# One written order replaced by another: squares and casts leave GpSimd, and one more output pair is made in seven products

## The chip, the cores and the metric

The kernel runs on one core of a Trainium2 chip. A core has five engines that run side by side: TensorE (PE in the profile) multiplies matrices, VectorE (DVE) and ScalarE (ACT) work element by element, GpSimd (POOL) does so too, more slowly, and starts DMAs, and SyncE (SP) does nothing here but start DMAs. Each engine works through its own list of instructions strictly in order; between engines, an instruction waits on semaphores until what it reads is there and what it overwrites is no longer needed. TensorE reads SBUF (the on-chip memory) and writes PSUM, eight banks of 2 KB in each of 128 partitions.

The metric is the device time of one execution in microseconds (us).

## The reference, cut to what matters

```
scores = q @ k.T / sqrt(64)                       # 8 batches, 12 heads, 448 positions, head size 64
attn   = maximum(scores, 0)**2 / 448
x      = (attn @ v), heads side by side           # 3584 tokens x 768
h      = x @ w_in                                 # 768 x 2048
out    = (h * sigmoid(1.702 * h)) @ w_out         # 2048 x 768, result 3584 x 768, float32
```

There is no softmax: a score is clipped at zero and squared, so the attention needs no row sums. All scale factors are put off: one factor 64*448 is divided out inside the activation of `h` and multiplied back when the activation is widened, and divided out again at the output.

## The kernel before, in words

**Units and groups.** The attention is cut into 24 units u = 0..23: three for each batch, four heads in each. The tokens are cut into eight groups g = 0..7 of 384 (even g) or 512 (odd g); a group's second stage can begin when the attention of its tokens is done. 128 tokens make a block m of the output; groups have three or four of them.

**The order is written out by hand** as one long string of words (line 466 on); `do` (line 441) reads a word and issues its instructions. The place of a word in the string sets the order on every engine and queue at once, since each engine takes its own instructions in the string's order. `:d`, `:a`, `:p` put a word on VectorE, ScalarE or GpSimd; without it the table `home` (line 439) decides, and what is not in the table is VectorE's. `@4.5` names the PSUM banks. The words that matter here:

- `Lk` `Lq` (line 97): load float32 k or q of a unit into `kst` or `qst` through SyncE; there is one buffer of each. `K` `Q` (line 107): cast it to 16 bit. `Rk` `Rq` (line 117): transposing DMA through SyncE into `kT`, `qT`. Units 0 to 5 are transposed on TensorE instead (`tk` `tq`, copied out by `ek` `eq`); for units 1 to 5 `jk` `jq` load and cast in one DMA through GpSimd. `V` loads v the same way (four buffers).
- `s u.j` (line 143): four score matmuls into two banks. `r u.j.a` (line 156): clip one bank into `at` (eleven buffers). `x u.j` (line 165): square `at`, 128 x 896, in place; both inputs of that product lie in SBUF. `a u` (line 173): 28 matmuls with v. `e` (line 189): copy the attention's result out as the group's input.
- `f g.f.r` (line 221): plain matmuls of the first layer (all of group 0, half of group 1), two at a time. `u g.i.n` (line 269): one of the seven products that make a 2 x 2 block of the first layer, six matmuls. `t`, `b` copy and add its partial sums, `g` applies the activation (ScalarE), `v` widens the result to 16 bit (line 216, GpSimd): the group's input of the second layer.
- `p g.m.n` (line 375): one of the seven products that make output blocks m and m+1, eight matmuls of 384 columns. `A g.m.n` (line 357) makes the sums of its left sides, `W c.n` (line 345) those of its right sides from `w_out`. `m` (line 337) makes half an output block plainly, 16 matmuls; `i` (line 399) does so with the weights that the sums have changed in place. `h`, `l`, `n` copy the results out, `o` stores them through SyncE.
- `S i.n` (line 245) and `T g.n` (line 259) make the sums for the first layer's products. `jwa` `jwb` (line 411) load `w_in` in four quarters of two halves, `jo` (line 415) loads `w_out`, all through GpSimd. `z` are matmuls of zeros at the start. `G3` (line 421) is a tiny copy on SyncE that waits for the last half but one of `w_in`, so that no `Lk`, `Lq` starts before it.

The sums with two operands (`tt`, line 87) are all on line 88, the widenings on line 217, the casts and copies on lines 79 to 85, the matmuls of the products on line 203.

Of the kernel before, what the change touches and what calls it, by code (L numbers as in the profile page):

```python
# [15 lines left out]
def kernel(  # L16
# [406 lines left out]
    with tc.manual_schedule():  # L423
# [15 lines left out]
        home = {"K": "a", "Q": "p", "r": "a", "t": "a", "h": "a", "v": "p"}  # L439
# [19 lines left out]
        def zeros(e, p, n):  # L459
# [8 lines left out]
            "Lk0 z13@0 jk1 V1 jq1 I V0 K0:d tk0@1 z1 ek0 jk2 Lq0 Q0:a tq0@2 eq0 tk1@3 s0.3@4.5 "  # L468
            "r0.3.1 jq2 ek1 s0.1@6.7 r0.1.0 r0.3.0:d s0.0@0.1 s0.2@2.3 tq1@5 r0.0.1:d r0.2.0 "
            "s0.5@4.6 r0.1.1 s0.4@1.2 r0.0.0 r0.5.1 s0.6@7.0 eq1 r0.4.0:d tk2@5 x0.0 s1.0@1.6 "  # L470
            "r0.4.1 x0.4 jwb2 r0.5.0 x0.5 r0.6.1 jk3 r0.2.1 r0.6.0 x0.3:p jq3 x0.1 ek2 r1.0.1 "
            "r1.0.0 x0.2 x0.6 s1.5@2.4 s1.2@0.3 r1.2.0 s1.1@7.6 r1.1.1 tq2@5 a0@1.0 r1.1.0 r1.5.0 "
            "s1.6@6.7 eq2 r1.2.1 x1.0 r1.5.1 r1.6.0 s1.3@5.2 r1.3.0 x1.1 x1.2 tk3@3 e0.0.0 "
            "e0.0.1:a jk4 x1.5 e0.1.0:a tq3@4 r1.3.1 ek3 eq3 jwb0 x1.3 jq4 jwa0 s1.4@6.5 r1.6.1 "
            "V2 x1.6 r1.4.1 r1.4.0 s2.0@1.3 s2.2@2.7 r2.2.1 e0.1.1:a s2.1@4.5 r2.0.1 r2.0.0 "
            "r2.2.0 tk4@6 r2.1.1 x1.4 a1@7.0 e1.0.1:a ek4 r2.1.0:d x2.2 s2.6@3.6 r2.6.0 tq4@1 "
            "r2.6.1 e1.0.0 s2.3@2.4 r2.3.0 e1.1.1 x2.0 x2.1 eq4 s2.4@5.0 r2.3.1 jwa1 s2.5@3.6 "
            "f0.2.0@2 r2.4.0 r2.4.1 jwb1 jwa2 jq5 f0.3.0@4 s3.0@1.5 x2.6 e1.1.0 x2.3 f0.3.1 x2.4 "
            "jk5 r2.5.0 r2.5.1 x2.5 r3.0.0:d S0.1 V3 f0.2.1 f0.0.0@7 f0.0.1 s3.1@0.3 r3.0.1 "
            "a2@6.5 jwb3 r3.1.1:d r3.1.0 s3.2@1.0 e2.0.0 f0.1.0@3 e2.0.1:a r3.2.1 r3.2.0 G3 "  # L480
            "e2.1.1:a e2.1.0 x3.0 f0.1.1 f0.1.2 g0.1 x3.1:p V4 f0.2.2 s3.5@6.0 r3.5.0:d g0.2 "
            "s3.4@1.5 f0.0.2 v0.1 f0.3.2 r3.4.0 V5 r3.4.1 f0.4.0@3 r3.5.1:d x3.2 x3.5 g0.3 g0.0 "
            "f0.4.1 s3.3@2.6 s3.6@1.0 jwa3 f0.8.0@5 r3.3.1 r3.6.0 v0.0 r3.3.0 f0.4.2 g0.4 f0.8.1 "
            "f0.8.2 s4.1@4.7 s4.3@6.1 r3.6.1:d s4.0@0.2 f0.6.0@3 f0.6.1 r4.1.0 r4.3.1 x3.6 V9 "
            "f0.6.2 r4.3.0 x3.3 f0.5.0@4 r4.1.1:d r4.0.1:d x3.4 f0.5.1 S0.2 x4.1 f0.5.2 v0.4 "
            "s4.2@7.1 x4.3 a3@2.6 g0.8 g0.5 r4.2.1:d s4.4@5.4 r4.2.0 r4.0.0 tq5@7 g0.6 v0.2 jo1.0 "
            "Lk6 r4.4.0:d r4.4.1 tk5@0 eq5 s4.5@1.3 s4.6@4.5 ek5 e3.0.1:a f0.11.0@6 x4.2:a "
            "f0.7.0@7 f0.11.1 f0.11.2 r4.6.1:d r4.5.0 r4.5.1:d r4.6.0:d f0.10.0@0 f0.10.1 f0.7.1 "
            "x4.6 e3.0.0:a jo0.0 x4.5:a x4.4 f0.10.2 S2.1 g0.11 s5.1@1.5 s5.0@2.3 x4.0:p v0.5 "
            "f0.7.2 v0.11 f0.14.0@4 r5.0.1:d v0.6 f0.14.1 g0.10 r5.1.0 r5.1.1 r5.0.0 f0.14.2 "  # L490
            "jo0.1 S1.1 g0.14 g0.7 s5.4@6.0 a4@1.3 s5.3@5.2 r5.4.0:d v0.7 r5.3.0 e4.0.0:a "
            "s5.2@4.7 r5.4.1:d r5.2.1:d f0.12.0@6 x5.0:p e4.0.1:a f0.13.0@0 r5.2.0:d f0.12.1 "
            "f0.12.2 x5.4:a g0.12 v0.3 f0.15.0@5 f0.15.1 s5.5@7.1 r5.5.1 s5.6@4.3 r5.3.1:d x5.3 "
            "r5.5.0:d r5.6.0:d f0.13.1 r5.6.1 jo1.1 f1.7.0@2 f0.13.2 f1.1.0@6 x5.1:p v0.12 v0.10 "
            "v0.14 K6:p x5.5:a g0.13 f0.15.2 f1.5.0@1 f1.5.1 f1.7.1 S2.2 S2.4 x5.2:a x5.6:a "
            "f0.9.0@7 f0.9.1 f0.9.2 f1.4.0@3 S2.3 g0.15 g0.9 a5@4.0 e5.0.1:a f1.0.0@5 f1.0.1 "
            "f1.3.0@7 f1.1.1 Lq6 Q6:a e5.0.0 T1.1 T1.2 S1.2 v0.13 f1.7.2 g1.7 f1.3.1 v1.7 v0.9 "
            "Lq7 f1.3.2 f1.4.1 f1.4.2 f1.5.2 Rk6 u1.2.0@0 f1.6.0@4 Rq6 S3.1 g1.5 f1.6.1 g1.3 "
            "f1.2.0@2 f1.0.2 f1.6.2 v1.3 v0.15 t1.2.0 S3.3 g1.0 v0.8 g1.6 v1.0 Lk7 T1.4 S3.2 g1.4 "
            "u1.2.2 S3.4 W2.1 f1.2.1 f1.2.2 S1.4 u1.3.0@1 v1.4 W1.1 Q7:a f1.1.2 g1.1 v1.5 v1.1 "  # L500
            "u1.2.1@7 b1.2.1 g1.2.1 v1.2.1 v1.6 m0.0.0@5 u1.2.3 g1.2 s6.2@4.3 T1.3 Lq8 t1.3.0 "
            "s6.1@6.2 u1.3.2 S0.3 t1.2.2 n0.0.0:a r6.2.0 u1.2.4 r6.1.1:d r6.2.1:d s6.0@5.4 r6.0.1 "
            "r6.0.0 x6.0:a t1.3.2 V11 t1.2.4:d W0.1 u1.3.1@2 W2.2 Rq7 W0.2 m0.0.1@3 K7:p Q8:a "
            "b1.3.1 b1.2.3 g1.2.3 Rk7 u1.2.5 u1.2.6 u1.3.4 r6.1.0 W3.1 S0.4 v1.2 V7 u1.3.3 g1.2.5 "
            "v1.2.3 s6.4@4.5 s6.3@6.0 S1.3 n0.0.1 t1.3.4 g1.3.1 b1.2.6 b1.3.3 s6.5@3.7 r6.4.0 "
            "u1.3.5 x6.1:p r6.3.0:d r6.4.1:d r6.5.0 W1.2 v1.3.1 v1.2.5 u1.3.6 Lk8 g1.3.5 W3.2 V6 "
            "x6.4:a r6.3.1:d x6.2:a r6.5.1 Rq8 b1.3.6 K8:p m0.1.0@4 s6.6@6.3 W2.4 v1.3.5 g1.3.3 "
            "v1.3.3 s7.2@5.1 g1.2.6 x6.3 W1.4 v1.2.6 Lq9 g1.3.6 s7.0@0.2 r7.2.1 r7.0.0 x6.5:a Q9 "
            "r6.6.1:d r7.2.0:d Lk9 r7.0.1 m0.1.1@7 r6.6.0:d n0.1.0:a Rk8 s7.1@3.1 x6.6 W3.4 "
            "x7.0:a a6@5.0 s7.3@6.2 r7.1.0:d r7.1.1 n0.1.1 Lq10 s7.4@4.3 x7.2 e6.0.1:a K9:p "  # L510
            "r7.3.1 e6.1.1:a e6.0.0 r7.4.0:d p1.0.0@1 o0.0 r7.4.1:d e6.1.0:a s7.6@7.2 s7.5@0.5 "
            "r7.3.0 x7.1 x7.3 r7.6.0 r7.6.1:d r7.5.0 s8.2@4.6 m0.2.0@3 r7.5.1 r8.2.0:d V10 x7.4 "
            "s8.1@7.0 x7.6 r8.2.1 x7.5:a h1.0.0 n0.2.0:a s8.0@5.6 r8.1.1 a7@2.4 v1.3.6 r8.0.1 "
            "A1.0.1@0 A1.0.2@1 s8.3@3.0 W0.4 r8.3.0 r8.1.0:d e7.0.1 e7.1.1:a r8.3.1 p1.0.1@6 "
            "s8.5@7.3 V8 e7.0.0:a r8.0.0:d x8.1 e7.1.0 r8.5.0:d Rk9 r8.5.1 Rq9 s8.6@4.5 x8.0 x8.2 "
            "r8.6.1 x8.3:a p1.0.2 x8.5 r8.6.0:d s8.4@0.2 r8.4.1 s9.0@3.7 r8.4.0 l1.0.1 r9.0.0 "
            "x8.6 r9.0.1 x8.4 x9.0:a m0.2.1@5 n0.2.1:a s9.1@2.4 A1.0.4 r9.1.1:d Lk10 r9.1.0 "
            "a8@0.3 s9.2@7.5 e8.0.0:a Q10:d e8.0.1:a s9.3@4.2 r9.2.1:d r9.3.1 K10:p p1.0.3 "
            "u2.0.0@5 r9.2.0 Rk10 u2.1.0@2 Lk11 K11:p T2.1 W3.3 e8.1.0 T2.2 T2.3 e8.1.1:a "
            "s9.4@7.3 u2.0.1@0 W1.3 r9.4.1:d t2.0.0 u2.0.2 b2.0.1 t2.1.0 u2.1.2 u2.1.1@3 r9.3.0:d "  # L520
            "b2.1.1 W0.3 T2.4 r9.4.0 t2.0.2 u2.0.3 u2.0.4 g2.0.1 v2.0.1 t2.1.2 u2.2.0@7 g2.1.1 "
            "t2.0.4 b2.0.3 Lq11 t2.2.0 v2.1.1 u2.1.4 t2.1.4 h1.0.2 x9.2 u2.1.3 b2.1.3 u2.2.1@4 "
            "u2.0.6 g2.0.3 v2.0.3 b2.2.1 x9.4:a u2.2.2 u2.1.6 b2.0.6 g2.2.1 g2.0.6 Rq10 W2.3 "
            "u2.2.3 u2.3.0@0 Q11:a b2.1.6 t2.2.2:d u2.0.5 v2.0.6 g2.1.6 u2.3.1@3 g2.1.3 t2.3.0:d "
            "b2.3.1 v2.1.6 v2.2.1 u2.2.4 u2.1.5 u2.3.2 u2.3.3 t2.2.4 u2.2.5 A1.0.3 b2.2.3 u2.2.6 "
            "Lk12 o0.1 g2.3.1 t2.3.2 v2.3.1 v2.1.3 g2.0.5 g2.1.5 v2.0.5 u2.3.4 p1.0.4 g2.2.3 "
            "g2.2.5 s9.6@5.2 v2.1.5 b2.2.6 s9.5@4.7 t2.3.4:d u2.3.5 x9.1:a v2.2.3 K12 Lq12 b2.3.3 "
# [147 lines left out]
```

## Time and profile before

Four executions took 369.32, 369.71, 372.15 and 372.30 us; the median is 370.93. The profiled one is the third.

| | profiled execution |
|---|---|
| device time | 372.15 us |
| span from the first to the last instruction | 370.4 us |
| granted TensorE clock | 0.994 of full speed |
| PE busy | 356.9 us, 3570 matmuls |
| DVE busy | 289.3 us, 519 instructions |
| ACT busy | 277.1 us, 542 instructions |
| POOL busy | 179.0 us, 229 instructions |
| DMA | 51.39 MB |

Busy time counts when at least one instruction of the engine is under way; neighbours on one engine overlap at their ends, so an instruction's own duration is longer than the step from one to the next. A row "A 0.55" of the timeline gives the start and then the time until the end. Matmuls are pipelined, so PE is shown busy also where matmuls trickle; the step from the start of one batch of matmuls to the next tells more than its busy share.

### The profile page before, as it was taken

The numbers are of one execution on the slowest core, as the hardware profiler recorded it, in microseconds if no ns is written. First come the engines' busy times: TensorE is split into PE (matmuls) and PEld (weight loads), VectorE is DVE, ScalarE is ACT, GpSimd is POOL, SyncE is SP. The second block draws the span as 40 slices with busy tenths as digits, with TensorE's granted clock in tenths as the row PEclk, the third lists the DMA queues.
The fourth block names the chain that finished last, engine by engine and source line by source line (L and its number), as shares of the span: only waits on it lengthen the run. The fifth ranks groups of instructions, "written<-read, shape, count | busy, mean of one in ns | idle before, by whom it ended". The sixth has DMA issues, their size and how long they took to land.

```text
span 370.4 us, 9086 instructions
## 1 busy us (share of the span) xinstructions
PE 356.9 (96%) x3570; PEld 231.0 (62%) x3570; DVE 289.3 (78%) x519; ACT 277.1 (75%) x542; POOL 179.0 (48%) x229
## 2 busy tenths in 40 slices
PE   7689999999999999999999999999999999999994
PEld 3344554674559655786559655786549755787662
DVE  4879997499998777878899678766887899764642
ACT  3968985688788988878977997888995897175310
POOL 6745685766213587257403765368342546043300
PEclk9989999999999999999999999999999999999999
DMA  9999999698984895978494396356934042300244
GB/s 197 184 202 186 213 208 191 159 193 198 132 158 112 187 254 99 162 166 193 96 195 89 95 170 165 101 141 152 245 88 88 2 112 27 87 0 2 64 118 118
DMA packets 65227, 51.39 MB, mean 139 GB/s; under 512 B 35744, under 2 KB 61856, under 8 KB 65184
## 3 DMA queue, kind: packets, MB, share of 16 engines
q1 hardware_dynamic: 48256, 36.32, 41.1%
q0 software_dynamic: 16608, 14.09, 26.2%
q8 instruction: 28, 0.46, 0.5%
q10 hardware_dynamic: 320, 0.39, 0.4%
q14 instruction: 15, 0.12, 0.1%
HBM read 45.61 MB, written 11.01 MB: 153 GB/s over the span
## 4 chain that ended last, share of the span: by engine, by line
PE 86%; DVE 6%; DMA 4%; POOL 2%; issue 1%; ACT 0%; SPq 0%; POOLq 0%; DVEq 0%; ACTq 0%
PE hx L203 29%; PE ox L203 26%; PE sc L150 9%; PE av L181 7%; PE ht L228 7%; PE os L203 4%; PE op L203 3%; DMA q<-in_q_dram 2%; DVE at L161 2%; DVE wT L88 1%; DVE at L88 1%; DMA qst<-in_q_dram 1%; PE tr L131 1%; DVE asum L88 1%; POOL at L88 1%
## 5 line engine op out<-in xcount | busy, mean ns | idle before, releaser
L163 ACT ACTIVATE at<-sc 128x448 f16<-128x448 f32 x215 | 105.0, 559 | 15.7 <-PE sc L150 15.4
L161 DVE TENSOR_SCALAR at<-sc 128x448 f16<-128x448 f32 x121 | 71.6, 616 | 12.9 <-PE sc L150 12.3
L217 POOL TENSOR_SCALAR go<-gf 128x512 f16<-128x512 f32 x64 | 41.3, 645 | 63.6 <-ACT gf L214 46.8
L88 DVE TENSOR_TENSOR gf<-hx,gf 128x512 f32<-128x512 f32 (+1 forms) x78 | 47.9, 626 | 26.8 <-PE hx L203 14.2
L203 PEld LDWEIGHTS <-win 128*128 128x128 f16 x624 | 56.4, 98 | 8.4 <-issue 2.8
L88 POOL TENSOR_TENSOR at<-at 128x896 f16<-128x896 f16 x27 | 45.8, 1700 | 30.8 <-ACT at L163 18.7
L217 POOL TENSOR_SCALAR ge<-gf 128x384 f16<-128x384 f32 x64 | 35.9, 561 | 46.1 <-ACT gf L214 28.9
L169 ACT ACTIVATE at<-at 128x896 f16<-128x896 f16 x57 | 53.9, 955 | 0.9 <-DVE at L161 0.6
L150 PE MATMUL sc<-qT,kT 64*64 64x448 f16 x672 | 51.3, 362 | 1.4 <-DVE at L161 0.6
L88 DVE TENSOR_TENSOR at<-at 128x896 f16<-128x896 f16 x84 | 51.9, 651 | 0.8 <-ACT at L163 0.4
L214 ACT ACTIVATE gf<-gf 128x512 f32<-128x512 f32 (+1 forms) x78 | 43.2, 580 | 9.4 <-DVE gf L88 9.3
L203 PE MATMUL ox<-wout,go 128*128 128x384 f16 x256 | 46.5, 327 | 0.0
L203 PEld LDWEIGHTS <-winS 128*128 128x128 f16 x468 | 42.6, 98 | 4.5 <-issue 1.0
L203 PEld LDWEIGHTS <-go 128*128 128x128 f16 x320 | 29.9, 98 | 22.6 <-issue 4.8
L203 PEld LDWEIGHTS <-ge 128*128 128x128 f16 x288 | 27.5, 98 | 19.7 <-issue 3.3
L79 ACT ACTIVATE gf<-hx 128x512 f32<-128x512 f32 (+1 forms) x51 | 27.3, 543 | 15.2 <-PE hx L203 7.2
L203 PE MATMUL hx<-T,winS 128*128 128x256 f16 (+1 forms) x312 | 37.0, 260 | 0.0
L181 PE MATMUL av<-at,v 64*64 64x448 f16 x672 | 36.6, 354 | 0.1
L150 PEld LDWEIGHTS <-kT 64*64 64x64 f16 x672 | 17.6, 105 | 25.9 <-issue 20.6
L203 PE MATMUL hx<-xo,win 128*128 128x256 f16 x252 | 32.1, 273 | 0.0
L203 PE MATMUL ox<-wT,asum 128*128 128x384 f16 x176 | 31.8, 327 | 0.0
L203 PEld LDWEIGHTS <-asum 128*128 128x128 f16 x200 | 18.7, 98 | 15.3 <-issue 3.1
(78 smaller groups left out, 482.6 us busy)
## 6 DMA issues: line engine op xcount, KB each, us to landing
out_dram<-osb SPq DMA_DIRECT2D x52, 192.0 KB, 3.2
kst<-in_k_dram SPq DMA_DIRECT2D x19, 448.0 KB, 4.7
qst<-in_q_dram SPq DMA_DIRECT2D x19, 448.0 KB, 4.0
v<-in_v_dram POOLq DMA_DIRECT2D x24, 224.0 KB, 5.4
win<-in_moe_w_in_dram POOLq DMA_DIRECT2D x8, 384.0 KB, 11.0
wout<-in_moe_w_out_dram POOLq DMA_DIRECT2D x4, 768.0 KB, 12.5
k<-in_k_dram POOLq DMA_DIRECT2D x5, 224.0 KB, 8.3
q<-in_q_dram POOLq DMA_DIRECT2D x5, 224.0 KB, 9.0
```

Of the source, the lines that this page charges most:

```text
L79: nc.scalar.activation(out=o, in_=i, func=AF.Copy)
L88: eng[e].tensor_tensor(out=o, in0=x, in1=y, op=op)
L131: nc.tensor.matmul(out=ps[64 * a:64 * a + 64, j * 128:(j + 1) * 128], lhsT=x[:, a, 64 * j:64 * j + 64], rhs=ident[:, :], is_transpose=True)
L150: nc.tensor.matmul(out=sc[a][c, 0:S], lhsT=st["kT"][r, j, c], rhs=st["qT"][r, :, c], start=True, stop=True)
L161: nc.vector.tensor_scalar(out=o, in0=i, scalar1=0.0, scalar2=None, op0=ALU.max)
L163: nc.scalar.activation(out=o, in_=i, func=AF.Relu)
L169: nc.scalar.activation(out=at, in_=at, func=AF.Square)
L181: nc.tensor.matmul(out=av[s][64 * a:64 * a + 64, 0:S], lhsT=v16[r, a, 64 * j:64 * j + 64], rhs=at[r, a, :], start=(j == 0), stop=(j == J - 1))
L203: nc.tensor.matmul(out=o, lhsT=lhs(i), rhs=rhs(i), start=start and i == 0, stop=i == n - 1, skip_group_check=True)
L214: nc.scalar.activation(out=o, in_=i, func=AF.Gelu_apprx_sigmoid, scale=1.0 / SC)
L217: eng[e].tensor_scalar(out=o, in0=i, scalar1=SC, scalar2=1.0, op0=ALU.mult, op1=ALU.mult)
L228: nc.tensor.matmul(out=hp[g, f][:, 0:n], lhsT=w[:, i, fo:fo + 128], rhs=xts[g][:, i, 0:n], start=i == 0, stop=i == NK - 1)
```

## The change

Nothing of the functions is changed, only the string of words, and one entry of `home`: a `Q` without an engine is ScalarE's. Over the whole string:

| | before | after |
|---|---|---|
| squares `x` on ScalarE, VectorE, GpSimd | 57, 84, 27 | 62, 106, 0 |
| casts `K` on ScalarE, VectorE, GpSimd | 6, 1, 12 | 16, 3, 0 |
| casts `Q` on ScalarE, VectorE, GpSimd | 8, 1, 10 | 16, 3, 0 |
| clips `r` on ScalarE, VectorE | 215, 121 | 223, 113 |
| copies `e` on ScalarE, VectorE | 40, 32 | 35, 37 |
| `h` on ScalarE, VectorE | 20, 13 | 23, 13 |
| `l` on ScalarE, VectorE | 6, 38 | 3, 45 |
| `n` on ScalarE, VectorE | 9, 3 | 4, 4 |
| plain half blocks `m`, `i` | 6, 6 | 0, 8 |
| products `p` and sums `A` | 77, 47 | 84, 52 |

All other words are there as often as before. The 128 widenings and all of GpSimd's DMAs stay where they were. The six `m` were group 0's three output blocks; now blocks 0 and 1 are seven products `p0.0.n`, and block 2 is two `i`. The order of nearly all words is new. The core of the diff (the opening, the last quarter of `w_in`, the first products of group 0 with unit 6 and 7 beside them, and the casts of units 17 and 18):

```diff
-        home = {"K": "a", "Q": "p", "r": "a", "t": "a", "h": "a", "v": "p"}
+        home = {"K": "a", "Q": "a", "r": "a", "t": "a", "h": "a", "v": "p"}
...
-            "Lk0 z13@0 jk1 V1 jq1 I V0 K0:d tk0@1 z1 ek0 jk2 Lq0 Q0:a tq0@2 eq0 tk1@3 s0.3@4.5 "
-            "r0.3.1 jq2 ek1 s0.1@6.7 r0.1.0 r0.3.0:d s0.0@0.1 s0.2@2.3 tq1@5 r0.0.1:d r0.2.0 "
-            "s0.5@4.6 r0.1.1 s0.4@1.2 r0.0.0 r0.5.1 s0.6@7.0 eq1 r0.4.0:d tk2@5 x0.0 s1.0@1.6 "
...
-            "f0.4.1 s3.3@2.6 s3.6@1.0 jwa3 f0.8.0@5 r3.3.1 r3.6.0 v0.0 r3.3.0 f0.4.2 g0.4 f0.8.1 "
...
-            "u1.2.1@7 b1.2.1 g1.2.1 v1.2.1 v1.6 m0.0.0@5 u1.2.3 g1.2 s6.2@4.3 T1.3 Lq8 t1.3.0 "
-            "s6.1@6.2 u1.3.2 S0.3 t1.2.2 n0.0.0:a r6.2.0 u1.2.4 r6.1.1:d r6.2.1:d s6.0@5.4 r6.0.1 "
-            "r6.0.0 x6.0:a t1.3.2 V11 t1.2.4:d W0.1 u1.3.1@2 W2.2 Rq7 W0.2 m0.0.1@3 K7:p Q8:a "
...
+            "jq1 Lk0 K0:d I jk1 Lq0 jwb2 Q0:a z13@0 tk0@1 jk2 ek0 tq0@2 tq1@3 eq0 s0.6@4.5 eq1 "
+            "s0.1@6.7 r0.1.0:d jq3 s0.3@1.2 z1 r0.3.1:d jq2 r0.6.0 tk1@3 s0.4@0.4 jk3 r0.6.1 V0 "
+            "r0.1.1:d r0.3.0 s0.0@6.5 r0.0.1 s0.2@2.1 r0.2.0:d ek1 r0.0.0 s1.1@7.5 jwa0 tk2@6 "
+            "r0.4.1 s1.0@2.4 r0.2.1 x0.3 x0.0 x0.6 s0.5@3.1 r1.1.1:d x0.1:a r0.4.0 x0.2 r1.1.0 "
...
+            "f0.8.0@4 e2.1.1 x3.3 r3.1.0:d f0.8.1 f0.8.2 V4 s4.1@5.1 s3.5@6.0 e2.1.0:a g0.2 g0.8 "
+            "s3.6@3.2 x3.1 r4.1.1:d r4.1.0 r3.5.0 f0.4.0@7 f0.6.0@4 s4.3@1.5 r3.5.1:d r3.6.0 "
+            "r3.6.1 r4.3.1:d s3.4@6.0 x3.5:a f0.6.1 v0.8 r3.4.1:d r3.4.0:d f0.4.1 x3.4 f0.6.2 "
+            "f0.4.2 x3.6:a g0.6 tq5@3 tk5@2 eq5 s4.2@5.0 V5 ek5 s4.0@6.4 g0.4 r4.0.1:d r4.2.1 "
+            "r4.2.0 r4.0.0:d a3@3.7 s4.5@2.0 s4.4@5.4 S0.1 v0.2 jwa3 f0.10.0@6 f0.10.1 jo1.0 "
+            "r4.4.1:d x4.2:a e3.0.1 f0.10.2 r4.5.0 r4.4.0 r4.3.0 x4.4 e3.0.0:a s4.6@2.4 r4.6.1:d "
+            "x4.1 S3.1 s5.2@5.7 r5.2.0 g0.10 r4.5.1 f0.7.0@1 x4.3 v0.6 jo0.0 f0.11.0@3 f0.7.1 "
+            "v0.1 f0.7.2 x4.0 r5.2.1 jo0.1 f0.5.0@5 f0.5.1 s5.1@4.6 g0.7 v0.7 s5.4@0.7 x4.5:a "
+            "r5.1.0:d f0.5.2 r5.4.1:d Lk6 r4.6.0 x4.6 f0.11.1 f0.11.2 f0.13.0@1 f0.13.1 s5.0@4.2 "
...
+            "S3.3 v1.2 v1.3 v1.5 u1.2.2 A0.0.1@0 W2.1 W3.1 W3.2 W0.1 Rk6 f1.0.1 f1.0.2 p0.0.0@1 "
+            "K7 g1.0 u1.3.0@3 s6.0@0.4 g1.6 W3.4 W2.2 W1.1 s6.2@2.7 t1.2.2 T1.3 Lq8 u1.2.4 v1.6 "
+            "h0.0.0 b1.2.1 W2.4 r6.0.1 t1.3.0 v1.4 W1.2 t1.2.4 r6.2.1 Q8 r6.0.0 r6.2.0 v1.0 W1.3 "
+            "p0.0.1@4 W3.3 u1.2.5 u1.2.3 u1.3.2 u1.3.1@7 s6.1@0.2 W0.2 g1.2.5 A0.0.2@1 g1.2.1 "
+            "W2.3 v1.2.1 b1.2.3 g1.2.3 t1.3.2 Lk8 r6.1.0 b1.3.1 u1.2.6 v1.2.5 r6.1.1 l0.0.1 Lq7 "
+            "b1.2.6 p0.0.2 Q7 W1.4 Rk7 s6.5@6.0 S0.3 s6.3@5.2 r6.5.0 W0.3 Rq8 u1.3.3 x6.0:a K8 "
+            "A0.0.3 r6.5.1:d r6.3.0:d u1.3.4 Rq7 t1.3.4:d r6.3.1 h0.0.2 x6.2 g1.3.1 p0.0.3 W0.4 "
+            "s6.6@6.0 s6.4@5.2 r6.4.1:d b1.3.3 r6.6.1 r6.4.0 x6.3 p0.0.4 v1.3.1 V8 x6.5:a A0.0.4 "
+            "h0.0.4 l0.0.3 u1.3.5 u1.3.6 g1.3.5 v1.3.5 b1.3.6 g1.3.3 p0.0.5 Lq9 x6.1 Lk9 s7.4@0.2 "
+            "r6.6.0 x6.6 x6.4 g1.2.6 s7.0@5.3 p0.0.6 s7.2@6.7 l0.0.5:a g1.3.6 r7.4.0 r7.0.0:d "
+            "r7.0.1:d r7.4.1 l0.0.6 r7.2.1 s7.1@1.0 r7.2.0 r7.1.0:d r7.1.1 v1.3.6 Rk8 x7.0 a6@5.2 "
...
+            "u4.0.0@7 t4.0.0:d u4.1.0@4 r15.2.0:d u4.2.0@2 u4.0.1@5 Lq17 T4.4 u4.0.2 t4.1.0 "
+            "h3.0.2 u4.1.1@1 T4.3 x15.0 b4.0.1 t4.0.2 u4.1.2 b4.1.1 Lk18 A3.2.1@0 u4.0.4 g4.1.1 "
+            "e14.1.0 t4.1.2 u4.0.3 t4.0.4:d Q17 g4.0.1 K18 Rk16 v4.1.1 x15.3 p3.0.4 b4.0.3 Lk19 "
```

Of the two casts in the last piece, `Q17` was GpSimd's before and stood apart from its load, and `K18` was ScalarE's.

## The prediction

> **What bounds the kernel now.** I read the page first, then TensorE's timeline, because the page's busy share of PE is no measure of work.
>
> ```profile
> span 370.4 us, 9086 instructions
> ...
> PE 356.9 (96%) x3570; PEld 231.0 (62%) x3570; DVE 289.3 (78%) x519; ACT 277.1 (75%) x542; POOL 179.0 (48%) x229
> ...
> PE 86%; DVE 6%; DMA 4%; POOL 2%; issue 1%; ACT 0%; SPq 0%; POOLq 0%; DVEq 0%; ACTq 0%
> ```
>
> The chain of waits runs through PE for 86% of the span. Starts in PE's timeline give the step of each batch:
>
> ```profile
> 77.64 0.82 PE L203 MATMUL hx<-T,win 128*128 128x256 f16 x6
> 78.30 0.82 PE L203 MATMUL hx<-xo,winS 128*128 128x256 f16 x6
> ...
> 91.06 0.54 PE L150 MATMUL sc<-qT,kT 64*64 64x448 f16 x5
> 91.87 0.38 PE L150 MATMUL sc<-qT,kT 64*64 64x448 f16 x3 [0.28 <-DVE at L161]
> ```
>
> One `u` of an odd group takes 0.66 (start to start), one of an even group 0.50; read the same way, a `p` takes 1.30, an `m` or `i` 2.60, an `s` 0.19, an `a` 1.32, an `f` 0.33 or 0.43, and a change from full products to `s` and back costs about 0.2. Summed over the string these steps make 333 us from the first first-layer product (`f0.2.0`, 27.5) to PE's last end (365.7), which lasted 338.2: PE waits there for about 5 us in all. Before it, from the first transpose at 4.9, it has 12 us of work in 22.6: 10.5 of waiting. After it come 4.7 us of last add and store. So the kernel can lose PE work, about 5 us of waits and part of 10.5 at the start, no more; it can gain waits without limit.
>
> Where PE waits after the start, the chain names VectorE's sums of `w_out`, at twice their usual length:
>
> ```profile
> 82.28 2.53 DVE wT L88 x2
> ...
> 87.36 1.20 DVE wT L88
> ```
>
> The timelines of VectorE and GpSimd beside it show why:
>
> ```profile
> 77.47 0.55 DVE L88 TENSOR_TENSOR wT<-wout,wout 128x768 f16<-128x768 f16 x1
> 77.94 0.55 DVE L88 TENSOR_TENSOR winS<-win,winS 128x768 f16<-128x768 f16 x1
> ...
> 82.20 2.61 DVE L88 TENSOR_TENSOR wT<-wout,wT 128x768 f16<-128x768 f16 x2
> ```
> ```profile
> 81.28 1.32 POOL L217 TENSOR_SCALAR go<-gf 128x512 f16<-128x512 f32 x2
> ...
> 83.45 0.94 POOL L83 CAST k<-kst 128x896 f16<-128x896 f32 x1
> 84.48 2.40 POOL L217 TENSOR_SCALAR go<-gf 128x512 f16<-128x512 f32 x3
> ```
>
> A sum that takes a step of 0.47 alone (77.47 to 77.94) takes some 1.2 while GpSimd widens or casts.
>
> **The change, part by part** (in us against the profiled execution).
>
> *PE work.* Four `m` of blocks 0 and 1 (4 x 2.60 = 10.4) give way to seven `p` (7 x 1.30 = 9.1): -1.3. The new order has some three changes between `s` and full products more: +0.3. Together **-1.0**, sure.
>
> *Work taken from GpSimd.* Busy time by count from these rows:
>
> ```profile
> L163 ACT ACTIVATE at<-sc 128x448 f16<-128x448 f32 x215 | 105.0, 559 | 15.7 <-PE sc L150 15.4
> L161 DVE TENSOR_SCALAR at<-sc 128x448 f16<-128x448 f32 x121 | 71.6, 616 | 12.9 <-PE sc L150 12.3
> L88 POOL TENSOR_TENSOR at<-at 128x896 f16<-128x896 f16 x27 | 45.8, 1700 | 30.8 <-ACT at L163 18.7
> L169 ACT ACTIVATE at<-at 128x896 f16<-128x896 f16 x57 | 53.9, 955 | 0.9 <-DVE at L161 0.6
> L88 DVE TENSOR_TENSOR at<-at 128x896 f16<-128x896 f16 x84 | 51.9, 651 | 0.8 <-ACT at L163 0.4
> ```
>
> ScalarE gets 8 clips (3.9), 5 squares (4.7), 18 casts at 0.95 (17.1) and 3 `h` (1.5), and loses 5 `e`, 5 `n`, 3 `l` (-6.4): +21, to 298. VectorE gets 22 squares (13.6), 4 casts (2.5), 5 `e`, 7 `l`, one `n` and 5 `A` (10.5), and loses 8 clips (-4.7): +22, to 311. GpSimd falls to 112. Against a span of 370 both still fit, so on average PE hides them; what counts is the stretches where VectorE is already full:
>
> ```profile
> 27.50:48.00 20.50, 20.50 (x228) 10.32 (x231) 20.25 (x37) 18.20 (x41) 12.44 (x17) 1.00 1.17 201
> 88.00:108.00 20.00, 19.51 (x212) 10.15 (x211) 19.67 (x38) 15.91 (x35) 5.08 (x7) 1.00 0.95 161
> ```
>
> (Columns: length, then PE, PEld, DVE, ACT, POOL busy.) With GpSimd's squares and casts goes the lengthening shown above. The 80 to 92 us stretch has 1.7 of PE's waits; all those named after the start make 2.8. I take **-1.7**, bounds -2.8 and 0, since widenings remain.
>
> *The new first pair, and the order around it.* Four `A0.0` sums are new, and all 16 `W` now stand ahead of `p0.0.4`; before, the last (`W2.3`) stood among group 2's first products. From `s6.0` to `a6` the new string has for PE 11 `s`, six `p`, ten `u`: 11 x 0.19 + 7.8 + 6.6, with five changes 17.4 us. For VectorE it has 39 instructions: 12 `W`, one `S`, one `T` at 0.47, 3 `A` and 6 `b` and a `t` at 0.60, 6 clips and 6 squares at 0.53, 3 `l` at 0.46: 20.4. That is 3.0 too much, with no widening in its way yet. Before, the same stretch had 14.5 for PE and 13.4 for VectorE. Part can run early, for VectorE has only some 4 us of work in the 10 before. The first PE words to suffer are `u1.3.5` and unit 7's scores, and behind those the whole of PE's list. Counted the same way elsewhere, the lists come near to PE's without passing it by much (from `a21` to `a23` ScalarE 14.4 on 15.7, where before it had 12.0). Bounds: nothing, if queues smooth it all as they now do where VectorE is 99% busy; +6 if each surplus is paid. I take **+2.5**, near the one surplus that is plain.
>
> *Casts on ScalarE.* A cast that comes before its load holds what is queued behind it; on GpSimd that was widenings, on ScalarE it is clips and activations. `Lq17` stands 2.5 us of PE steps ahead of `Q17`, `Lk18` 1.0 ahead of `K18`; SyncE can reach them at most 3 us ahead (its stores of `o2.2` stand before). The loads land after 4.0 and 4.7 us by the page. So ScalarE stands for about 2 us at group 4's first products, with `g4.0.1` between the casts and the later copies and clips behind. `K14`, `Q7`, `K10` have 4 to 5.5 us. PE has other products in its list meanwhile: bounds 0 and +3.5, I take **+0.8**.
>
> *Opening.* The same loads must land before `f0.2.0` as before, with a DMA share of 1.13 for 27.5 us. Waits for q1, k2 and q3 (1.4, 1.0 and 1.5 of idle PE) ease, as scores of units 0 and 1 now stand between; but v0, issued at 4.2 and used at 15.0 before, now stands behind `jk3`, which needs `tk1`: it starts at about 10 and lands, at 5.4 us for the median v and up to 9 for a load in this stretch, at 15 to 19, and `a0` holds the eleven `at` buffers until then. Bounds -1.5 and +1.5, taken **0**.
>
> *Last quarter of `w_in`.* `jwa3` to `f0.13.0` was 14 us of PE steps; now it is 5, about 9 from where GpSimd can reach it. These loads take 5.8 to 12.8. **+0.3**, bounds 0 and +3.5.
>
> GpSimd's queue otherwise runs ahead sooner (no square before `V`); SyncE's transposing DMAs keep at least 6.6 us to their first score, for 4 to 5 to land.
>
> Sum: -1.0 - 1.7 + 2.5 + 0.8 + 0 + 0.3 = **+0.9**. The profiled execution took 372.15, 1.2 above the median of 370.93; on the median the forecast is **371.8**.
>
> [...]
>
> **Rivals.**
> *VectorE and ScalarE become the bound.* For it: the surplus of 3.0 above, and both together now average 82% of the span. Against it: PE hardly waited at 99% busy. Price: 3.0 there, 1 in the first 20 us of the first layer, 2 in all near units 15 and 22, 2 for casts and locks, less PE's 1.0 and the rest of GpSimd's waits: +6, 377. It decides once VectorE falls over 3 us behind, about what its list now holds in bursts.
> *Faster.* PE's waits fall with GpSimd's; the queues absorb the surplus: -1.0 - 1.7 - 1.5 at the start = -4.2, 366.7. For it: the chain names little else than those sums.
> *The late quarter.* `f0.13.0` waits the full 3.5: +0.9 - 0.3 + 3.5 = +4.1, 375.0.
> *It doesn't do what it says:* squares on VectorE wait for widenings as sums did; that is within the first rival's price.
>
> **How the numbers follow.** Forecast 0.50, bound by VectorE and ScalarE 0.27, faster 0.16, late quarter 0.07. The extremes of all bounds (-5.3, +13.5) would need everything at once; the range goes from 366.0, the faster case with a little more, to 377.5, just past the slower one. 1% is 3.7 us, about what a measurement of this kernel tells from no change: faster below 367.2 0.18, slower above 374.6 0.31, within 0.51. The likeliest case's own range is 368.5 to 374.5.
>
> **What would show it.** PE x3562; POOL near 112 busy, squares only on L88 DVE and L169; no `wT` sum beyond 0.9 us; PE's waits after 27 us at 60 to 80 us naming VectorE; ACT waiting for `qst` or `kst` near 205 us; `f0.13.0` near 46 us. I am wrong if the opening moves by over 1.5 us, or if PE's waits arise from banks of clips all along.

## The result and the profile after

The changed kernel takes 371.4 us (median of 48 executions, 368.92 to 377.41). The kernel before, run beside it, takes 369.38 (74 executions, 368.69 to 372.30). The ratio is 1.0033, with a 95% interval of 1.0019 to 1.0046: no difference by the 1% named above, and the forecast was 371.8. The forecast had started from 370.93, the median of four executions of before, 1.55 above that of the 74. (The comparison leaves out the twelve executions of after that lie over 1.5% above its fastest, which is why the ratio is below that of the medians, 1.0055; what makes them slow is the main finding below.) The profiled execution took 373.88, with a granted clock of 0.989.

The page of after, the lines that answer to those shown of before:

```profile
span 372.1 us, 9009 instructions
...
PE 359.5 (97%) x3562; PEld 232.8 (63%) x3562; DVE 301.0 (81%) x555; ACT 294.5 (79%) x563; POOL 113.3 (30%) x180
...
PE 89%; DMA 4%; ACT 2%; DVE 1%; POOL 1%; issue 1%; DVEq 0%; POOLq 0%
...
L163 ACT ACTIVATE at<-sc 128x448 f16<-128x448 f32 x223 | 110.3, 560 | 10.2 <-PE sc L150 9.6
L161 DVE TENSOR_SCALAR at<-sc 128x448 f16<-128x448 f32 x113 | 67.0, 615 | 6.5 <-PE sc L150 6.1
...
L88 DVE TENSOR_TENSOR at<-at 128x896 f16<-128x896 f16 x106 | 64.8, 629 | 3.8 <-ACT at L163 2.6
...
L169 ACT ACTIVATE at<-at 128x896 f16<-128x896 f16 x62 | 58.6, 959 | 1.8 <-DVE at L161 1.4
```

The chain has lost VectorE's 6% and keeps DMA's 4%: part of the latter is one load in the middle of the kernel. The chain of waits, in order of time (start, length, what), and then the two waits in it that matter, in VectorE's timeline and in PE's:

```profile
37.83 8.81 DMA win<-in_moe_w_in_dram
...
46.73 0.20 DVE winS L88
46.93 0.27 issue
47.20 1.46 DVE at L88 x2
48.66 1.08 DVE at L161 x2
49.74 0.04 issue
49.78 2.46 PE av L181 x28
```
```profile
46.73 0.56 DVE L88 TENSOR_TENSOR winS<-win 128x768 f16<-128x768 f16 x1 [2.53 <-DMA win<-in_moe_w_in_dram]
```
```profile
49.25 0.38 PE L150 MATMUL sc<-qT,kT 64*64 64x448 f16 x4 [1.67 <-DVE at L161]
```

The last quarter of `w_in` lands at 46.63. VectorE has stood still 2.53 us for it, at the sum `S3.1`; behind that sum in its list stand two squares and the clips that free PE's banks. PE waits 1.67 us at `s5.0`. And then 28 matmuls with v take 2.46 us in the chain (2.18 from their start to that of the next batch), where a step of `a` is 1.32. The table by stretches says why (length, then PE, PEld, DVE, ACT, POOL busy with the number of instructions, granted clock, DMA share, GB/s):

```profile
12.66:16.07 3.41, 2.06 (x31) 0.88 (x27) 3.14 (x7) 3.38 (x8) 0.05 (x1) 1.00 1.14 175
16.07:19.48 3.41, 3.19 (x38) 1.72 (x40) 3.19 (x7) 3.41 (x7) 3.41 (x5) 0.50 1.25 202
46.79:50.20 3.41, 1.59 (x20) 0.81 (x24) 3.41 (x7) 2.19 (x4) 1.76 (x2) 1.00 1.30 209
50.20:53.62 3.42, 3.42 (x35) 1.72 (x28) 3.15 (x8) 1.38 (x4) 0.00 (x0) 0.50 1.32 204
```

The granted clock falls to one half for 3.41 us, right after a stretch of 3.41 us in which PE was thinly busy. The two starts, 16.07 and 50.20, lie ten times 3.41 us apart. Each such half-clock stretch costs up to 1.7 us, an estimate: half its length, if PE is busy all through it. So the late quarter is paid twice: PE's batches from 46 to 54 us run 4.0 us behind their steps.

Over all executions whose clock is listed, the lost clock carries most of the difference of the medians. "Lost" is (1 - granted clock) x span:

| | executions | median us | mean lost us | median of (time - lost) |
|---|---|---|---|---|
| before | 92 | 369.60 | 0.7 | 369.0 |
| after | 49 | 371.48 | 2.8 | 369.25 |

Among the 49 of after, the 16 with a clock of 0.9965 or more have a median of 370.0, the 13 from 0.992 on 371.2, the 12 from 0.987 on 373.5, the 8 below 375.0. A straight line through them rises by 1.03 us for each us of lost clock. Of before, 79 of the 92 have such a clock of 0.9965 or more, with a median of 369.5. So with a full clock 0.6 us of the difference of 1.9 is left, and by the last column of the table 0.25. The loss is an upper bound of what it costs: in the profiles of before and after the clock falls to one half once more behind PE's last matmul, at 369.4 and 371.1 us, where nothing waits for it (e1's mean clock of 0.993 leaves room for 1.8 us of that beside its one stretch, h0's of 1.00 for hardly any).

### The profile page after: what moved, and what is told of

Read it like the earlier page. It is cut to its first block, busy times and chain, and to the rows that moved or that the text cites. A ratio compares the mean times of both kernels' runs of the same rounds, so it can differ in the third digit from the quotient of the medians.

```text
span 372.1 us, 9009 instructions
## 1 busy us (share of the span) xinstructions
PE 359.5 (97%) x3562; PEld 232.8 (63%) x3562; DVE 301.0 (81%) x555; ACT 294.5 (79%) x563; POOL 113.3 (30%) x180
## 4 chain that ended last, share of the span: by engine, by line
PE 89%; DMA 4%; ACT 2%; DVE 1%; POOL 1%; issue 1%; DVEq 0%; POOLq 0%
PE ox L203 30%; PE hx L203 29%; PE sc L150 9%; PE av L181 8%; PE os L203 6%; PE ht L228 5%; DMA win<-in_moe_w_in_dram 2%; DMA q<-in_q_dram 2%; PE zp L463 1%; ACT at L163 1%; PE tr L131 1%; POOL ge L217 1%; DVE at L88 0%; DVE at L161 0%; POOL v L104 0%
## 5 line engine op out<-in xcount | busy, mean ns | idle before, releaser
L163 ACT ACTIVATE at<-sc 128x448 f16<-128x448 f32 x223 | 110.3, 560 | 10.2 <-PE sc L150 9.6
L161 DVE TENSOR_SCALAR at<-sc 128x448 f16<-128x448 f32 x113 | 67.0, 615 | 6.5 <-PE sc L150 6.1
L217 POOL TENSOR_SCALAR go<-gf 128x512 f16<-128x512 f32 x64 | 42.7, 667 | 90.5 <-ACT gf L214 87.9
L88 DVE TENSOR_TENSOR at<-at 128x896 f16<-128x896 f16 x106 | 64.8, 629 | 3.8 <-ACT at L163 2.6
L88 DVE TENSOR_TENSOR gf<-hx,gf 128x512 f32<-128x512 f32 (+1 forms) x78 | 47.8, 625 | 23.5 <-PE hx L203 12.8
L169 ACT ACTIVATE at<-at 128x896 f16<-128x896 f16 x62 | 58.6, 959 | 1.8 <-DVE at L161 1.4
L181 PE MATMUL av<-at,v 64*64 64x448 f16 x672 | 38.2, 362 | 0.3
L203 PEld LDWEIGHTS <-ge 128*128 128x128 f16 x256 | 24.0, 98 | 18.7 <-issue 4.3
L203 PE MATMUL ox<-wT,asum 128*128 128x384 f16 x192 | 34.7, 327 | 0.0
L203 PEld LDWEIGHTS <-asum 128*128 128x128 f16 x224 | 21.1, 98 | 15.9 <-issue 2.1
L181 PEld LDWEIGHTS <-v 64*64 64x64 f16 x672 | 21.5, 110 | 12.6 <-issue 3.0
```

The lines of the kernel that those rows point to most:

```text
L88: eng[e].tensor_tensor(out=o, in0=x, in1=y, op=op)
L161: nc.vector.tensor_scalar(out=o, in0=i, scalar1=0.0, scalar2=None, op0=ALU.max)
L163: nc.scalar.activation(out=o, in_=i, func=AF.Relu)
L169: nc.scalar.activation(out=at, in_=at, func=AF.Square)
L181: nc.tensor.matmul(out=av[s][64 * a:64 * a + 64, 0:S], lhsT=v16[r, a, 64 * j:64 * j + 64], rhs=at[r, a, :], start=(j == 0), stop=(j == J - 1))
L203: nc.tensor.matmul(out=o, lhsT=lhs(i), rhs=rhs(i), start=start and i == 0, stop=i == n - 1, skip_group_check=True)
```

## The experiments

### The late quarter: three ways to take its price away

`e1_s31_late` and `e2_jwa3_early` each move one word of after; `e3_zero_fill` leaves the wait and fills PE's gap with matmuls of zeros.

```diff
 e1:  - x4.1 S3.1 s5.2@5.7 ...  r5.4.0:d S3.2 a4@7.3
      + x4.1 s5.2@5.7 ...       r5.4.0:d S3.1 S3.2 a4@7.3
 e2:  - jwb3 r3.2.1:d ...       v0.2 jwa3 f0.10.0@6
      + jwb3 jwa3 r3.2.1:d ...  v0.2 f0.10.0@6
 e3:  + f0.13.1 y0.13.10 s5.0@4.2     # ten matmuls of zeros into f0.13's open sum
```

> The kernel after, with one word moved: VectorE's sum S3.1, the first that reads the last quarter of w_in, stands directly ahead of S3.2 instead of after x4.1. Theory (the late quarter, paid twice): in the profile of after VectorE stands 2.53 us at S3.1 until the quarter lands at 46.63, PE then waits 1.7 us for clips, and the granted clock is 0.50 from 50.2 to 53.6, which costs another 1.7. With S3.1 later none of it is left: no VectorE wait for w_in over 0.5 us, PE's waits from 46 to 54 us under 1.2 us in sum (4.0 in after), granted clock 1.00 in 45 to 60 us, median 2 to 3 us below after's 371.4: 368.9 or less. Rival (VectorE's and ScalarE's load): the clips are late by their own number, the waits only move to the next scores and the median stays within 0.7 of 371.4.

> The kernel after, with one word moved: the DMA jwa3 of the last quarter of w_in stands right behind jwb3 on GpSimd's list, instead of behind V4, V5 and two widenings. It is then issued near 26.5 instead of 37.8 us and lands near 39. Theory (the late quarter): as for the run before, no wait of VectorE at S3.1, no half clock near 50 us, 368.9 or less; V4 and V5 land up to 1.5 us later, which nothing near 49 us waits for. Rival (load of VectorE and ScalarE): within 0.7 of 371.4. If it differs from the run before by over 1 us, the DMA's other neighbours matter.

> The kernel after, with ten matmuls of zeros (128x384, 0.16 us each) added on PE between f0.13.1 and s5.0, where PE stands still 1.7 us; they add zero to the open sum of f0.13. The waiting for VectorE stays. Theory (the stall costs a second time through the granted clock): VectorE's wait of about 2.5 us for w_in stays, PE waits at s5.0 for under 0.5 us, the granted clock stays 1.00 from 46 to 60 us, and the median falls by 0.8 to 1.7 from 371.4, since the half-clock stretch goes but the stall itself does not. Rival (the clock's fall has nothing to do with that stall, or costs nothing): the median stays at 371.4 or rises by up to 1.6, the fill's own length.

Measured: e1 370.39 (ratio to before 1.0008, 0.9989 to 1.0028), e2 370.96 (1.0028, 1.0003 to 1.0053), e3 371.77 (1.0047, 1.0022 to 1.0071), 12 executions each. In the profiles of e1 and e2 VectorE no longer waits for `win`, PE's waits from 46 to 54 us are gone, and the clock is 1.00 from 20 to 78 us (0.993 and 0.999 in the mean of the whole span). With the lost clock taken off, the medians are 368.4 for both against 369.25 of after: the stall itself is worth about 0.9 us over all executions, an estimate. The executions with a clock of 0.9965 or more say about the same, but are few: 369.4 in e1 (four) and 369.1 in e2 (two), against 370.0 in after. But the medians fell by 1.0 and 0.4 only, not by the 2 to 3 expected, since 8 of 12 and 10 of 12 executions still have a clock below 0.9955: there is another source of half-clock stretches; in e1's profile one lies from 16.1 to 19.5 us. e3 told nothing: in its profile VectorE waited just 0.7 us for the quarter and the clock was 1.00 up to 78 us (0.997 in the mean), and where the low clock lay in 8 of its 12 executions is not on record.

### The engines: squares and casts alone

`f1` gives the 27 squares back to GpSimd in the new order (with `S3.1` late). `h1` does the opposite: it takes them from GpSimd in the old order, to the engines of after; `h2` takes the casts as well.

```diff
 f1 (from e1):  - x17.5      + x17.5:p     # and 26 more
 h1 (before):   - x17.5:p    + x17.5       # and 26 more: 18 VectorE, 9 ScalarE
 h2 (h1):       - K11:p      + K11:a       # and 21 more casts: 20 ScalarE, 2 VectorE
```

> The first run's kernel (S3.1 late), with the 27 squares that the change took from GpSimd given back to it, at their places in the new order. Theory (GpSimd's squares lengthened VectorE's two-input sums, and PE paid 1.7 us for it): slower than the first run by 1 to 2.5 us, sums of w_out again near 1.2 us while a square of GpSimd runs, PE waits near 80 to 92 us back. Rival (VectorE and ScalarE are short of time, so the squares were better on GpSimd): faster than the first run by 1 us or more. If both are within 0.7, the squares' engine matters to neither.

> The kernel before with one part of the change alone: its 27 squares on GpSimd go to the engines they have in after (18 to VectorE, 9 to ScalarE), at their places in the old order. Theory (what the prediction gave for it): VectorE's sums of w_out beside GpSimd shorten, PE's waits of 80 to 92 us (1.7) go, VectorE and ScalarE take the squares beside PE: 1 to 2 us faster than before. Rival (VectorE becomes the bound where it was 99% busy): slower by 1 to 4, PE waiting for clips of VectorE in 27 to 48 or 88 to 108 us.

> The run before and the 22 casts of k and q on GpSimd as well, to ScalarE (20) and VectorE (2), as in after, in the old order. Theory (prediction): each cast is as long on ScalarE, one or two of them wait there for a load and hold clips: 0 to 1 us slower than the run before this one. Rival (20 us more on ScalarE are too much): 2 us or more slower than it. If it is faster than it, GpSimd's casts were in the way of VectorE's sums just as the squares were.

Measured: f1 392.3 (ratio 1.0595, 1.0559 to 1.0632), h1 375.2 (1.0153, 1.0123 to 1.0183), h2 386.95 (1.0468, 1.0431 to 1.0505). All three are far slower: f1 on the side of the theory, but about ten times its price, h1 and h2 on the side of the rivals and beyond the 1 to 4 us named for h1. In these two orders each choice of engines fits only the order written for it.

f1 first. GpSimd's timeline, and two steps of the chain of waits beside it:

```profile
238.50 1.96 POOL L88 TENSOR_TENSOR at<-at 128x896 f16<-128x896 f16 x1 [3.52 <-DVE at L161]
240.41 0.78 POOL L104 DMA_DIRECT2D v<-in_v_dram  x1
```
```profile
240.41 3.68 DMA v<-in_v_dram
...
244.12 2.07 PE av L181 x17
```

GpSimd waits 3.52 us for a clip of the square's input, squares for 1.96, and only then issues the load of v that PE's next products need: PE stands 4.3 us at `a17`, and another 3.4 at `a20` in the same way, and the clock is one half for 10.2 us around and behind the two (0.95 in the mean from 200 to 300 us). In the new order nothing kept such loads clear of GpSimd's squares, since it has none.

Nor did anything keep VectorE's own work clear of them. Beside the same square of GpSimd, a sum of VectorE that takes 0.68 alone (0.68 and 0.69 in after) takes three times as long (VectorE's timeline):

```profile
238.84 2.17 DVE L88 TENSOR_TENSOR ge<-ge 128x1024 f16<-128x1024 f16 x1
```

Twelve squares of VectorE run beside one of GpSimd in f1; their median is 1.71 us, against 0.62 alone, and together they take 11.4 us more. In the profile of before there are three, and 1.1 us. How f1's 22 us divide among the late loads, the clock and VectorE is not shown. The sums of `w_out`, which the theory named, stay at 0.97 or less in f1.

In h1 the lengthened sums of `w_out` are still there though no square is left on GpSimd (VectorE's timeline, then GpSimd's):

```profile
80.48 2.56 DVE L88 TENSOR_TENSOR wT<-wout,wT 128x768 f16<-128x768 f16 x2
```
```profile
80.80 0.94 POOL L83 CAST k<-kst 128x896 f16<-128x896 f32 x1
81.83 0.81 POOL L217 TENSOR_SCALAR go<-gf 128x512 f16<-128x512 f32 x1
```

So the squares were not what lengthened them, but what GpSimd does at that place, here a cast and a widening; PE's waits of 80 to 92 us stayed. In h2, where the casts have gone too, the same two sums take 1.42 together, and no `wT` sum takes more than 0.96 (VectorE's timeline of h2):

```profile
80.87 1.42 DVE L88 TENSOR_TENSOR wT<-wout,wT 128x768 f16<-128x768 f16 x2
```

So the sums of 1.2 us and more go with the casts. The rest of h1's loss is many small waits of up to 1.2 us along the whole kernel, the largest 1.15 near 307 us: VectorE and ScalarE late.

h2 adds one wait that dwarfs the others (ScalarE's timeline, then PE's):

```profile
113.35 0.95 ACT L79 ACTIVATE k<-kst 128x896 f16<-128x896 f32 x1 [4.83 <-DMA kst<-in_k_dram]
```
```profile
114.46 0.58 PE L150 MATMUL sc<-qT,kT 64*64 64x448 f16 x3 [5.47 <-ACT xo L79]
```

ScalarE stands 4.83 us at a cast whose load has not landed, clips and copies behind it, PE stands 5.47, and the clock is one half from 112.5 to 119.3. This is the prediction's fourth term, in the old order: in after the same casts stand where their loads have landed.

### The opening and the clock

`h0` is the kernel before once more. `c1` is e2 with 14 matmuls of zeros where PE stands still in the opening. `d1` is e2 with an early load moved back, `d2` moves a transposing DMA as well, `d3` adds seven zeros to that. `g1` is c1 with a copy moved ahead of a clip.

```diff
 c1 (e2):  + Y8@5 s1.1@7.5 ...  Y6@3 tq2@3          # eight and six matmuls of zeros
 d1 (e2):  - Lq0 jwb2 Q0:a ...  jwa2 r1.6.0
           + Lq0 Q0:a ...       jwa2 jwb2 r1.6.0
 d2 (d1):  - Rq6 Lk7 ... Rk6    + Rq6 Rk6 Lk7
 d3 (d2):  + Y4@5 s1.1@7.5 ...  Y3@3 tq2@3
 g1 (c1):  - r0.2.0:d ek1       + r0.1.1:d ek1 ... r0.2.0:d    # and Y8 becomes Y4
```

> The kernel before, unchanged, for a second profile. Theory (each stretch at half the granted clock costs up to 1.7 us, and where it falls changes from execution to execution): if its granted clock is 0.997 or more, the first first-layer product f0.2.0 starts 1 to 2.5 us earlier than in the first profile (27.5) and the time is 369.5 or less; if there is a half-clock stretch again, it lies before 28 us and lasts 3.4 us. Rival (the clock does not matter to the time): f0.2.0 within 0.5 of 27.5 whatever the clock.

> The kernel after with jwa3 early (the second run), and 14 matmuls of zeros added on PE in the opening: eight ahead of s1.1 (bank 5), six ahead of the transposes of q2 (bank 3), where PE stands still for 1.4 us each. Theory (thin stretches of PE in the opening bring the half clock, and jwa3 early removes the later one): granted clock 0.997 or more in at least 9 of 10 executions, median 369.0 to 369.6, against 370.96 without the zeros. Rival (the spread of after comes from the loads, not from the clock): the median stays within 0.5 of 370.96.

> The kernel after with jwa3 early (the second run), and the DMA jwb2, half of w_in's third quarter, moved on GpSimd's list from third place, ahead of k2, q2, k3, q3 and all v, to behind jwa2. Theory (the new opening is longer because that load takes the place of loads that PE waits for): q2 lands near 12.5 instead of 15.1 us, the first-layer product f0.2.0 starts near 24 instead of 26.0, as in the undisturbed profile of before (23.8), fewer half-clock stretches, median 368.0 or less against 370.96. Rival (the opening is bound by the sum of all loads or by clips): f0.2.0 stays within 0.5 of 26.0 and the median within 0.7 of 370.96.

> The run before this one, and Rk6, the transposing DMA of unit 6's k, moved on SyncE's list from behind Lk7 to ahead of it. Theory (PE's wait for kT at s6.0, 1.5 us in the profile with S3.1 late, is a transfer held in SyncE's list): kT of unit 6 is issued 1 us or more earlier, no wait of PE for it, median lower by 0 to 0.6. Rival (the 12.8 us of that transfer are contention with w_out's loads, whatever its place): no change within 0.3.

> The run before this one, and seven matmuls of zeros in the opening (four ahead of s1.1, three ahead of the transposes of q2). Theory (the clock): fewer executions under a granted clock of 0.997 and a narrower spread; the lowest time rises by up to 0.5, the median falls by 0 to 0.7. Rival (with the loads early PE has no thin stretch left there): the zeros only cost time, median 0.3 to 1 higher.

> The kernel after with jwa3 early and zeros in the opening, and VectorE's copy ek1 of unit 1's transposed k moved ahead of one clip (r0.2.0); the zeros ahead of s1.1 go from eight to four, since the wait there shortens. Theory (the opening of after is longer because copies that PE waits for stand behind clips on VectorE, not because of the loads): s1.1 starts near 10.9 instead of 11.9 us, f0.2.0 0.5 to 1 earlier than in that run's profile (27.2), median 368.5 to 369.2 against 369.47. Rival (the opening is bound by the clips and squares themselves): the time that s1.1 gains is lost again at the next scores, f0.2.0 and the median within 0.3.

| | median us | ratio to before (95%) | executions with clock below 0.9955 |
|---|---|---|---|
| h0 | 368.90 | one execution | 0 of 1 |
| before | 369.60 | | 11 of 92 |
| after | 371.4 | 1.0033 (1.0019 to 1.0046) | 33 of 49 |
| e2 | 370.96 | 1.0028 (1.0003 to 1.0053) | 10 of 12 |
| c1 | 369.47 | 0.9995 (0.9976 to 1.0014) | 0 of 12 |
| d1 | 371.07 | 1.0039 (1.0020 to 1.0058) | 7 of 12 |
| d2 | 370.88 | 1.0032 (1.0009 to 1.0056) | 7 of 12 |
| d3 | 371.74 | 1.0069 (1.0041 to 1.0096) | 5 of 12 |
| g1 | 369.42 | 0.9984 (0.9962 to 1.0006) | 1 of 12 |

h0's mean clock was 1.00. The first rows of the first layer's products (durations in ns; first and last start in us) of h0 and of e2, whose profile had a clock of 0.999:

```profile
L228 PE MATMUL ht<-xe,win x96: 322/326/337, 23.8 to 52.9; 128*128 128x384 f16 x96
```
```profile
L228 PE MATMUL ht<-xe,win x96: 323/326/337, 26.0 to 56.9; 128*128 128x384 f16 x96
```

Without half-clock stretches the opening of before ends at 23.8, not at 27.5; that of after at 26.0. Other profiles without a half clock in the opening agree: 23.9 in h1 and 24.2 in h2, which have the opening of before but for one square, and 26.0 in e3 and d2, which have that of after or nearly. Of the 3.7 us between 27.5 and 23.8, where 1 to 2.5 were expected, the half clock can be at most 1.7, half of a stretch of 3.41. Counted by the steps, PE's waits in h0's opening come to 6.3 us, in e2's to 8.7, the two largest 1.45 at `s1.1` and 1.47 at the transposes of q2. The profile on which the prediction was built had a half-clock stretch from 21.3 to 24.7 us and longer waits for loads; the first profile of after had one from 16.1 to 19.5. So the two openings looked alike.

c1 puts zeros into those two gaps: all twelve clocks are 0.996 or more (nine at 0.997 or more), the median falls by 1.5 us and the spread shrinks from 3.7 to 0.9 us. That shows that thin PE in the opening brings the half clock, and that the half clock makes e2 slow. (The two ran on different chips; on these, before had a clock below 0.9955 in 3 of 29 and 3 of 17 executions. g1, with ten zeros and on a third chip, had it in 1 of 12.) The zeros are not free: `f0.2.0` starts at 27.2 in c1's profile.

What makes that opening 2.2 us longer was not found. It is not the early load: in d1's profile q2 still landed at 15.4, two half-clock stretches followed each other (13.7 to 20.6), and the time stayed; in d2's, which has the same move, q2 landed at 13.1 with the clock at 1.00, and `f0.2.0` still started at 26.0. The copy `ek1` behind VectorE's clips was not settled: in g1 `s1.1` starts at 11.2, where 10.9 was expected, and the median is that of c1, as the rival said. But 11.2 is also where it starts in e2, without zeros ahead of it; the 11.9 of c1 was the zeros' own delay. d2 changed nothing beyond its interval: PE's wait before `s6.0`, 1.4 us for kT in e1's profile, was already gone in d1's. That d3, with half of c1's zeros and the moves of d1 and d2, is the slowest of them was not expected. Its profile has a clock of 1.00 up to 78 us (0.997 in the mean) and shows a wait of its own:

```profile
36.81 0.82 PE L228 MATMUL ht<-xe,win 128*128 128x384 f16 x4 [2.18 <-DMA win<-in_moe_w_in_dram]
```

PE waits there for the second half of `w_in`'s second quarter (`jwa1`), which stands behind the moved load on GpSimd's list. It lands at 36.8 in d3, at 35.0 in d2, where PE stands 0.8 us at that place (the profile names a clip there as well), and at 34.0 in e2 and c1, where it does not. That the moved load delays it is likely, not tested.

No version beats the kernel before: e1, c1 and g1 equal it within their intervals.

## Why the prediction was right, and where it was not

The sum was +0.9 and 371.8; the time is 371.4. The number fits by luck: against 369.38, the median of before beside it, after takes 2.0 us more and not 0.9, and the base was 1.55 too high. The terms, against what the runs showed. The comparison is that of two profiles with a full clock, h0 (1.00) and e2 (0.999): 338.6 us from `f0.2.0` to PE's last end become 336.0 (336.0 as well in c1, d1 and g1).

| term | predicted | shown |
|---|---|---|
| PE work | -1.0 | -1.0 by the steps; PE x3562 as said |
| GpSimd's squares and casts gone | -1.7 | by the steps, PE's waits after `f0.2.0` fall from 5.7 to 4.3 in e2; of the reason given, the squares fail |
| new first pair | +2.5 | 0.6 in after: 0.16 before `p0.0.1`, 0.40 before `p0.0.4` |
| casts waiting for loads | +0.8 | 0 |
| opening | 0 | +2.2 with a full clock, and half-clock stretches besides |
| last quarter of `w_in` | +0.3 | about +0.9 over all executions, 4.0 in the profile |
| after PE's end | none | +0.5 (4.7 to 5.2) |
| half-clock stretches | none | mean lost 2.8 us against 0.7 |

*Work taken from GpSimd.* The size was about right, the cause half right. The step that failed in part is "With GpSimd's squares and casts goes the lengthening shown above". h1 takes the squares away and keeps the lengthening; h2 takes the casts too, and it is gone, in the old order. In the profile of before no square runs beside any of the twelve `wT` sums; the two longest, 1.89 and 1.28, run beside a cast, and beside widenings alone none takes more than 0.85. So the reading "some 1.2 while GpSimd widens or casts" holds for the casts. Yet h2 is no faster for it: between 80 and 92 us PE now waits 0.9 and 0.3 for ScalarE's clips. The new order stands ten of the twelve sums between 68 and 77 us, where most take their usual length, a few up to 0.96, even beside widenings (VectorE's timeline of after, where six widenings run from 71.2 to 76.6):

```profile
70.45 1.02 DVE L88 TENSOR_TENSOR wT<-wout,wT 128x768 f16<-128x768 f16 x2
71.39 0.96 DVE L88 TENSOR_TENSOR wT<-wout,wout 128x768 f16<-128x768 f16 x1
```

The casts cost 11.7 us (h2 against h1), though one takes 0.94 us on either engine (GpSimd in before, ScalarE in after); most of that is one wait for a load and its half clocks. A square took 1.70 us on GpSimd and 0.65 on VectorE in before, and yet the move of the squares alone is no gain (h1 is 5.8 slower than before). A faster engine that is full was not the better place here. VectorE's squares beside widenings cost little: in after 21 run beside one, and together they take 1.4 us more than their usual 0.62 each, against 0.7 in before. No run shows the "locks" in the first rival's price of "2 for casts and locks"; in their place stand these 1.4 us, and 0 for the casts.

*The new first pair.* The count of 20.4 us of VectorE on 17.4 of PE was sound, but the price was taken at nearly the whole surplus. VectorE was ahead: sums of `w_out` ran from 68 us on, before the stretch began, and PE waited 0.6. The bound "nothing, if queues smooth it all" was the better choice.

*Casts on ScalarE.* `Lq17` and `Lk18` landed at 199.1 and 200.4, their casts ran at 200.0 and 201.3, with nothing idle before them. The margin is 0.9 us; ScalarE came later than PE's steps said. The mechanism is real, and where it strikes it can cost more than the upper bound of 3.5, as h2's 5.47 us of PE shows.

*Last quarter.* The watch was on the wrong reader. `f0.13.0` started at 46.8, as foretold near 46, with 0.26 of waiting. But `S3.1` reads the same quarter, stands earlier in VectorE's list, and holds clips. The prediction asked what stands behind a PE word that waits for the load, and not what stands behind a sum of VectorE that does.

*Opening.* "Taken 0" failed by 2.2 us with a full clock, past the bound of 1.5.

*The signs.* Right were the counts (PE x3562, POOL 113.3 busy for 112, squares on L88 DVE and L169 alone) and `f0.13.0`. VectorE came out at 301 busy for 311, ScalarE at 294.5 for 298. The `wT` sums went to 0.96 for 0.9. PE's waits for VectorE at 60 to 80 us and ScalarE's near 205 us did not come. The opening, said to make the forecast wrong if it moved by over 1.5 us, did move; the two first profiles (27.5 and 27.1) hid it.

*What was missed altogether* is the clock. The granted clock of 0.994 stood in the table of before, and its half-clock stretch lies in the middle of the opening that the prediction compared. With a full clock the longer opening and end (+2.7) and the work and waits that went (-2.6) cancel: h0's span is 367.1 us, e2's 367.2. The late quarter and the clock then make after slower than before, and the base that was too high brings the forecast to the median: a right number with wrong terms. The rival of VectorE and ScalarE as the bound holds in the old order (h1: 375.2; h2: 386.95, though mostly by one late load), not in the new.

## What to carry to other kernels

Before two profiles are compared, compare their granted clocks by stretches of a few microseconds: a stretch at 0.50 shifts everything behind it, and where it falls changes from execution to execution (at 21.3 us in one profile of before, nowhere up to 300 us in the other). A stall of PE can cost more than its length: around 1.67 us of waiting PE was busy for 1.59 us of 3.41, and then the clock stood at 0.50 for 3.41 us, up to 1.7 us more by an estimate. Cheap matmuls of zeros in the gaps can buy the latter back (in c1, 1.5 us of the median against e2). With a late load, look for every reader on every engine, and for what stands behind each; and do not price an engine's relief apart from the order it runs in: the same squares cost 22 us on GpSimd in one order and save 5.8 there in the other.

## What was not expected of the hardware

- Clock 0.50 in stretches of 3.41 us (before: 21.27 to 24.68; after: 16.07 to 19.48 and 50.20 to 53.62) or of twice that (d1: 13.7 to 20.6). Ahead of each stretch of before and after PE was thinly busy: 1.41, 2.06 and 1.59 us of 3.41. It is no sharp limit by the busy time shown: before's first profile had 1.96 us busy from 7.62 to 11.03, and no half clock after it (1.00 from 11.03 to 14.44).
- The same kernel had none to three or four such stretches, an estimate from its mean clocks of 1.00 to 0.982: executions of after spread over 8.5 us, most of it with the clock (correlation 0.84). On one chip, e2's twelve had clocks from 0.999 to 0.987.
- Matmuls of zeros in PE's gaps kept the clock up (c1: no clock below 0.996 in twelve executions, against ten of twelve below 0.9955 without them).
- Two-input work of VectorE beside a square of GpSimd took several times its usual time (f1: squares of 0.62 us at 1.71 in the median of twelve, 2.79 at most).
